# Attention on query blocks of 64 by key blocks of 128, with fp16 transposes, 1 KB loads and attention steps spread between MLP units

## The chip, the cores and the metric

The kernel runs on one core of one Trainium2 chip. The metric is the device time of one execution in microseconds (us). Each quoted time is the median of several executions, with their range. The span of a run, from its first to its last instruction, is 1.6 to 1.9 us shorter than its time. The profiled execution of before is not among its timed runs: its span of 415.4 us points to a time of about 417 us (an estimate), 1% above the median, so a difference of spans against before is off by some 2 to 4 us from the difference of the medians. A single core has no second die to compare with, so a run is called slow when it lies over 1.5% above the fastest of the same kernel; all profiled runs here were fast (for before by that estimate).

The engines are PE (matrix multiplications and transposes), DVE (vector), ACT (activation, exponentials and casts), GpSimd (called POOL in the trace) and SP, which issues DMA transfers. PSUM is the memory into which these kernels let PE write its results, and from which DVE and ACT take them; the other tiles lie in SBUF. The granted clock is the share of PE's full clock that the profile reports as let through by the throttle.

## The reference

There are 8 batches, 8 heads, 576 tokens and 64 elements per head. Attention is causal with a window of 64 tokens. Its result goes through a normalisation and an MLP of 512 to 2,048 to 512, and the attention output is added again.

```
pos = arange(576); rel = pos[:, None] - pos[None, :]
mask = (rel >= 0) & (rel < 64)
attn = softmax(where(mask, q @ k.T / 8, -1e9));  x = attn @ v      # as [8, 576, 512]
xn   = (x - mean) / sqrt(var + 1e-6) * g_ln
out  = x + relu(xn @ w_ch1) @ w_ch2
```

The 4,608 tokens form 36 blocks of 128, and four blocks form an MLP group, so there are nine groups and eight batches of attention.

## The kernel before

All inputs are loaded as fp32. The q and k loads take 256-byte runs (one token of one head). PE transposes the fp32 data, and DVE casts while it takes the result out of PSUM:

```
def emit_tr_burst(b, c):                       # c: chunk of 128 tokens
    for hp in range(H // 2):                   # a pair of heads
        tp = p_ps_att.tile([128, 2, 128], FP32, tag="att", ...)      # pool of 6 PSUM buffers
        nc.tensor.transpose(out=tp[:, 0, :nr], in_=qn[:nr, 2*hp:2*hp+2, :], ...)
        nc.tensor.transpose(out=tp[:, 1, :nr], in_=kn[:nr, 2*hp:2*hp+2, :], ...)
        nc.vector.tensor_copy(out=qkT[(b, hp)][:, :, s0:s0+nr], in_=tp[:, :, :nr])
```

Scores take 128 keys by up to 192 queries. V is cast by DVE, w1 and w2 by ACT. The MLP of a group is queued as 16 first-layer units and four second-layer units, and the emission order puts one to three units after each attention step (`filler(n)`). The weights arrive in the order in which the MLP wants them, with attention for batches 0 and 1 between:

```
for c in range(NCH):
    emit_loads_qk(0, c)
wdma(0, 1, 2, 3)                # w1 pieces on SP
...                             # V of batch 0
for c in range(NCH):            # batch 0, with w1 loads and casts between its blocks
    ...
    emit_block_pv(kblk)
    if kblk == 0: wcast(0, 1)
    elif kblk == 1: wcast(2, 3); wdma(4, 5)
    ...
```

A scheduler in the compiler may reorder the instructions of an engine; what is called the compiled order below is the result.

The softmax here doesn't subtract the row's maximum and nothing guards it: scores larger than these inputs give would overflow.

## Time and profile before

| | before |
|---|---|
| time, median of 3 runs | 413.38 us (413.15 to 414.93) |
| span of the profiled run | 415.4 us |
| first MLP matmul | 49.7 us |
| last output addition of MLP groups 0 to 8 begins at | 105.6, 158.9, 200.9, 240.9, 281.5, 322.5, 356.2, 383.9, 411.6 us |

These lines of the page of before are the span, the busy time of each engine, the busy tenths in 40 slices of 10.4 us, and the shares of the chain of work that ended last (followed back from the last instruction, at each step to what released it).

```profile
span 415.4 us, 7242 instructions
PE 375.3 (90%) x2768; PEld 195.4 (47%) x2768; DVE 236.2 (57%) x820; ACT 161.1 (39%) x337; POOL 37.8 (9%) x50
PE   2576559769999999999999999999999999999996
PEclk9999979987969999999999999999999999999999
DMA  9999998991791951496139133920002001102002
PE 72%; DMA 10%; ACT 7%; SPq 6%; DVE 4%; issue 1%; ACTq 0%
```

The DMA row is at 9 in most of the first nine slices, while PE is at 2 to 9: the start waits for loads. From the tenth slice on, PE is at 9.

The next lines are busy time by stretch in before. The columns are the window, its length, and the busy time and instruction count of PE, PEld, DVE, ACT and POOL, then the granted PE clock, the DMA share and the bandwidth.

```profile
core 0: us, PE busy (x) PEld busy (x) DVE busy (x) ACT busy (x) POOL busy (x), PEclk, DMA share, GB/s
47.00:106.00 59.00, 48.29 (x306) 22.41 (x305) 25.21 (x88) 30.41 (x62) 4.22 (x5) 0.88 0.80 196
106.00:159.00 53.00, 52.31 (x409) 28.11 (x408) 38.11 (x140) 19.42 (x44) 4.22 (x5) 0.94 0.68 132
...
201.00:241.00 40.00, 39.72 (x332) 20.95 (x326) 28.49 (x94) 18.80 (x44) 2.47 (x3) 1.00 0.46 103
...
357.00:384.00 27.00, 27.00 (x127) 12.25 (x126) 2.14 (x4) 9.55 (x16) 0.00 (x0) 1.00 0.11 39
```

Group 0 falls into a stretch of 59 us, starved of weights and at a granted clock of 0.88. A middle group takes 40 us and PE is busy for 39.7 of them. A late group, with no attention left, takes 27.7 us by the table.

### The profile page before, as it was taken

What the parts mean: (1) busy time and instruction counts of PE and PEld (TensorE: products, weight loads), DVE (VectorE), ACT (ScalarE), POOL (GpSimd) and SP (SyncE); (2) the same over time, 40 slices, a digit from 0 to 9 for tenths busy, and PEclk for the clock granted to TensorE, in tenths of its full rate; (3) what the DMA queues carried; (4) which work ended last, traced back from release to release, by engine and by line L of the source; (5) the groups of instructions that cost most, each with busy time, mean ns of one, the idle gap of its engine ahead of it and who ended that gap; (6) DMA issues with size and microseconds to landing.
All of it is one profiled execution on the core that took longest, in us unless ns stands there. A gap on an engine that the chain in (4) does not pass through costs nothing.

```text
span 415.4 us, 7242 instructions
## 1 busy us (share of the span) xinstructions
PE 375.3 (90%) x2768; PEld 195.4 (47%) x2768; DVE 236.2 (57%) x820; ACT 161.1 (39%) x337; POOL 37.8 (9%) x50
## 2 busy tenths in 40 slices
PE   2576559769999999999999999999999999999996
PEld 1355324424545654564465456545644544444442
DVE  3387803564758856885697579748856717102001
ACT  1152248931066226423545333533380450440620
POOL 8232100210011001300010020000000000000000
PEclk9999979987969999999999999999999999999999
DMA  9999998991791951496139133920002001102002
GB/s 180 210 243 238 191 235 236 251 214 61 163 163 33 178 134 52 114 184 148 51 95 195 62 109 79 152 76 28 2 1 77 27 0 51 52 0 77 25 27 76
DMA packets 90227, 46.62 MB, mean 112 GB/s; under 512 B 79312, under 2 KB 79312, under 8 KB 90192
## 3 DMA queue, kind: packets, MB, share of 16 engines
q1 hardware_dynamic: 85328, 36.71, 39.8%
q0 software_dynamic: 2784, 8.92, 9.2%
q10 hardware_dynamic: 2080, 0.52, 0.7%
q8 instruction: 22, 0.36, 0.4%
q14 instruction: 13, 0.11, 0.1%
HBM read 36.70 MB, written 9.44 MB: 111 GB/s over the span
## 4 chain that ended last, share of the span: by engine, by line
PE 72%; DMA 10%; ACT 7%; SPq 6%; DVE 4%; issue 1%; ACTq 0%
SPq L89 3%; DMA w2st_945<-in_moe_w_ch_dram 2%; SPq L88 2%; DMA w1s_541<-in_moe_w_ch_dram 2%; DMA w1s_367<-in_moe_w_ch_dram 2%; DMA w1s_125<-in_moe_w_ch_dram 1%; ACT w2s L141 1%; DMA w1s_694<-in_moe_w_ch_dram 1%; PE ch_1_1160 L174 1%; DMA w1s_654<-in_moe_w_ch_dram 1%; PE ch_0_2539 L174 1%; PE ch_0_4513 L174 1%; PE ch_2_3334 L174 1%; PE ch_0_3240 L174 1%; PE ch_2_3982 L174 1%; PE ch_0_3888 L174 1%
## 5 line engine op out<-in xcount | busy, mean ns | idle before, releaser
L162 PEld LDWEIGHTS <-w1g 128*128 128x128 f16 x576 | 53.7, 100 | 62.5 <-issue 15.6
L174 PEld LDWEIGHTS <-hrT_630 128*128 128x128 f16 x64 | 6.8, 107 | 13.2 <-issue 7.6
L179 DVE TENSOR_TENSOR osb_5225<-ch_0_5208,xn_4120 128x512 f32<-128x512 f32 x1 | 0.7, 692 | 16.7 <-PE ch_0_5208 L174 16.7
L179 DVE TENSOR_TENSOR osb_5401<-ch_0_5384,xn_4743 128x512 f32<-128x512 f32 x1 | 0.7, 692 | 16.7 <-PE ch_0_5384 L174 16.7
L174 PEld LDWEIGHTS <-hrT_5013 128*128 128x128 f16 x64 | 6.3, 98 | 7.5
L174 PEld LDWEIGHTS <-hrT_4730 128*128 128x128 f16 x64 | 6.3, 98 | 7.6
L174 PEld LDWEIGHTS <-hrT_4422 128*128 128x128 f16 x64 | 6.2, 98 | 6.7 <-issue 0.2
L174 PEld LDWEIGHTS <-hrT_3834 128*128 128x128 f16 x64 | 5.9, 98 | 7.0 <-issue 0.5
L174 PEld LDWEIGHTS <-hrT_3186 128*128 128x128 f16 x64 | 5.9, 98 | 6.8 <-issue 0.5
L174 PEld LDWEIGHTS <-hrT_2608 128*128 128x128 f16 x64 | 5.9, 98 | 6.6 <-issue 0.5
L174 PEld LDWEIGHTS <-hrT_1416 128*128 128x128 f16 x64 | 6.0, 98 | 6.4 <-issue 0.5
L174 PEld LDWEIGHTS <-hrT_1980 128*128 128x128 f16 x64 | 5.9, 97 | 6.5 <-issue 0.7
L214 ACT ACTIVATE pt_0_1419<-sc_0_0_0_1420 128x384 f16<-128x384 f32 x1 | 0.5, 490 | 21.0 <-PE sc_0_0_1_1424 L207 21.0
L174 PE MATMUL ch_0_1104<-w2s,hrT_630 128*128 128x512 f16 x16 | 5.2, 439 | 3.4 <-ACT w2s L141 3.4
L166 ACT ACTIVATE hrT_4730<-hps_0_5112 128x512 f16<-128x512 f32 x1 | 0.6, 597 | 15.7 <-PE hps_0_5112 L162 15.7
L174 PE MATMUL ch_1_1160<-w2s,hrT_630 128*128 128x512 f16 x16 | 6.3, 522 | 0.0
L166 ACT ACTIVATE hrT_5013<-hps_0_5288 128x512 f16<-128x512 f32 x1 | 0.6, 597 | 14.1 <-PE hps_0_5288 L162 14.1
L179 DVE TENSOR_TENSOR osb_5049<-ch_0_5032,xn_3528 128x512 f32<-128x512 f32 x1 | 0.7, 690 | 9.4 <-PE ch_0_5032 L174 9.4
L195 DVE CAST qkT_2_547<-tp_2_2_682 128x256 f16<-128x256 f32 x1 | 0.4, 425 | 9.1 <-PE tp_2_2_682 L194 9.1
L214 ACT ACTIVATE pt_0_190<-sc_0_0_0_191 128x384 f16<-128x384 f32 x1 | 0.5, 490 | 12.5 <-PE sc_0_0_1_195 L207 12.5
L162 PE MATMUL hps_2_656<-zT_581,w1g 128*128 128x512 f16 x4 | 1.9, 622 | 3.8 <-ACT hrT_630 L166 3.8
L166 ACT ACTIVATE hrT_4422<-hps_0_4669 128x512 f16<-128x512 f32 x1 | 0.6, 597 | 11.8 <-PE hps_0_4669 L162 11.8
(2695 smaller groups left out, 1173.9 us busy)
## 6 DMA issues: line engine op xcount, KB each, us to landing
vnat_0_127<-in_v_dram ACTq DMA_DIRECT2D x1, 256.0 KB, 4.6
qnat_0_98<-in_q_dram SPq DMA_DIRECT2D x1, 256.0 KB, 4.0
knat_0_99<-in_k_dram SPq DMA_DIRECT2D x1, 256.0 KB, 5.7
vnat_1_129<-in_v_dram ACTq DMA_DIRECT2D x1, 256.0 KB, 6.5
vnat_2_140<-in_v_dram POOLq DMA_DIRECT2D x1, 256.0 KB, 7.4
qnat_1_102<-in_q_dram SPq DMA_DIRECT2D x1, 256.0 KB, 10.8
vnat_3_142<-in_v_dram POOLq DMA_DIRECT2D x1, 256.0 KB, 8.8
knat_1_103<-in_k_dram SPq DMA_DIRECT2D x1, 256.0 KB, 10.5
```

The costliest lines, as they stand in the source:

```text
L88: nc.sync.dma_start(out=qn[:nr], in_=q[b, :, s0:s0 + nr, :].rearrange("h s d -> s h d"))
L89: nc.sync.dma_start(out=kn[:nr], in_=k[b, :, s0:s0 + nr, :].rearrange("h s d -> s h d"))
L141: nc.scalar.activation(out=w2s[:, hc, :], in_=w_data.pop(p), func=AF.Copy, bias=0.0, scale=1.0)
L162: nc.tensor.matmul(out=hps, lhsT=w1g[:, kc, 128 * hc:128 * (hc + 1)], rhs=zt[:, kc, :], start=(kc == 0), stop=(kc == NKC - 1),)
L166: nc.scalar.activation(out=hrT[:, hc, :], in_=hps, func=AF.Relu, bias=0.0, scale=1.0)
L174: nc.tensor.matmul(out=ch, lhsT=hrT[:, hc, 128 * kb:128 * (kb + 1)], rhs=w2s[:, hc, :], start=(hc == 0), stop=(hc == NHC - 1),)
L179: nc.vector.tensor_tensor(out=o, in0=ch, in1=x_norm[kblk][:, :, :].rearrange("p h d -> p (h d)"), op=ALU.add,)
L195: nc.vector.tensor_copy(out=qkT[(b, hp)][:, :, s0:s0 + nr], in_=tp[:, :, :nr])
L214: nc.scalar.activation(out=ptc[:nk, s0:s0 + 2, :nq], in_=sc[:nk, :, :nq], func=AF.Exp, bias=0.0, scale=scale,)
```

## The change

The change is a rewrite of the attention part and of the emission order. Its intent is less attention work on PE, fewer and longer loads, fewer casts on ACT and DVE, and attention steps spread evenly between smaller MLP units. Its core, with cuts:

```diff
+# q, k: partition p holds the four tokens 4p..4p+3, so one run is 1 KB; GpSimd casts them to fp16
+nc.sync.dma_start(out=t[:, :].rearrange("p h j d -> p h (j d)"),
+    in_=src[b, hs, 0:512, :].rearrange("h (p j) d -> p h (j d)", j=4))
+# v and w2 are cast by the DMA itself
+nc.gpsimd.dma_start(out=vA[b][:nr, c, :, 0:D], in_=v[b, :, 128*c:128*c+nr, :].rearrange("h s d -> s h d"))
+# V shifted by 64 rows, so that 128 keys around a query block are one operand
+def make_vB(b):
+    nc.vector.tensor_copy(out=vB[b][64:128], in_=vA[b][0:64])
+    nc.vector.tensor_copy(out=vB[b][0:64, 1:5], in_=vA[b][64:128, 0:4])
-tp = p_ps_att.tile([128, 2, 128], FP32, tag="att")         # 6 buffers, shared
+tp = ps_t.tile([128, 2, 4, 128], FP16, tag="tp")           # 1 buffer for all transposes
+for i in range(2):
+    for j in range(4):
+        nc.tensor.transpose(out=tp[:, i, j, :], in_=src[:, i, j], identity=ident16)
+for i in range(2):      # undo the order of tokens: j is the fastest index of the destination
+    nc.vector.tensor_copy(out=dst[:, hp, 0:512].rearrange("c (p j) -> c j p", j=4), in_=tp[:, i])
 ...                    # scores: 64 queries by 128 keys; mask of 64 columns used for all
+for i in range(4): w2_load(i)
+load_v(1, range(5))                     # behind w2 on GpSimd's queue
+for st in att_steps(0, 0): st()         # the whole attention of batch 0, no MLP beside it
+for i in range(16): w1_cast(i)
+for g in range(NGRP):                   # 32 units of a group; steps of batch g+1 spread over 28
+    units = mlp_units(g); steps = att_steps(g + 1, g + 1); span = 28
+    ...
```

## The prediction

> **What bounds it now.** The core's summary says PE 90% busy. Read by stage (busy time per window, and order of time on PE):
>
> - 0 to about 105 us: loads. The slices show DMA at 90% or more until about 93 us at 180 to 250 GB/s; the chain of waits runs through the w1 and w2 loads. PE is half busy. MLP group 0 ends at 105.5 us.
> - 159 to 322 us (groups 2 to 5): PE, busy 98 to 100%. One group takes 40 to 41 us.
> - Last two groups, no attention left: 27.7 us each. So the MLP costs 27.7 us per group and attention adds 12 to 13 us of PE time.
>
> **What the change does to PE per group.** From the timeline of before, a batch costs: fp32 transposes of q and k (0.11 to 0.165 us each) 5 to 6 us, zT transposes 2.1 us, scores 2.1 us, PV 2.9 us (0.65 us a block). After: 40 fp16 transposes (estimate 0.06 to 0.1 us each, as their evacuation is now batched) 3 us, zT 1.3, scores 2.5 (72 matmuls of 64 columns in place of 40 of up to 192), PV 2.0 (always 16 matmuls a block). Estimate 9 to 10 us, plus 1 to 2 us of stalls, since PSUM has one buffer for transposes and one for PV. Period 38.5 us (36 to 41) in place of 40 to 41: small gain. DVE and ACT stay well below: I sum about 24 us of DVE work per group (1,024-element mask about 0.6 us, zT copies 1.1 us, q/k copies 0.6 us).
>
> **What it does to the start.** Fewer bytes are wanted early (batches 0 and 1 and the weights, 15.5 MB), in longer runs. But the compiled order holds a trap: DVE builds the shifted V of batch 1 before it evacuates the first transpose of batch 0, and waits for V of batch 1. That load stands on GpSimd's queue behind all of w2. So 6.6 MB of that queue must land while SP's queue (q, k, w1) competes. The Trainium skill, "DMA: Bandwidth & Descriptors", section "Issuing engines are not separate DMA queues", says that both run on the same 16 engines and interleave; the trace agrees: 200 to 240 GB/s together in the first 30 us. About 13 MB at 230 to 260 GB/s: DVE starts batch 0 near 50 us (42 to 60). Batch 0's attention is then unfilled, some 20 to 24 us of DVE chain, so MLP starts near 74 us (before: near 47 us). But from there w1, w2 and batch 1 are present, so no group starves: group 0 ends near 113 us and group 1 near 151 us (before: 105.5 and 159).
>
> **Sum.** 74 + 7 x 38.5 + 2 x 27.7 + 1 = 400 us, less 2 us as the timed run is shorter than the profiled span: 398 us. Range 380 to 418. Chances: faster 0.64, same 0.28, slower 0.08.
>
> **What would show it.** First DVE copy out of a transpose at 42 to 60 us, preceded by a wait for a V load; first MLP matmul at 62 to 85 us; distance between the ends of groups 2 to 6 at 36 to 41 us; last two groups again 27.7 us each; q/k transposes paced at 0.06 to 0.1 us; PE idle in group periods 1 to 3 us, released by DVE.
>
> **What would make it wrong.** Casting DMA slower (or faster) than plain loads, moving the start by 10 us or more; GpSimd's queue winning more than half of the bandwidth (start near 60 us, total near 385); GpSimd casts and DVE slowing each other; stalls at the single transpose buffer stretching the period beyond 41 us, which takes the gain away.

## More of the kernel before

The granted PE clock dips to 6 or 7 tenths in three single slices: the sixth, where PE is half busy, and the tenth and twelfth, where PE is at 9.

Group 1 takes 53 us although PE is busy for 52.3 of them: it holds the q and k transposes of two batches (80 of the 320; groups 2 to 5 hold one batch each, group 6 none) at a clock of 0.94.

In the trace in order of time, this is how DVE took q and k transposes out of PSUM in before. The columns are start, duration, engine, line, operation and shapes.

```profile
140.03 0.41 DVE L195 CAST qkT_1_1786<-tp_1_1_1819 128x256 f16<-128x256 f32 x1
140.36 0.41 DVE L195 CAST qkT_2_1787<-tp_2_1_1823 128x256 f16<-128x256 f32 x1
```

Each copy of 256 elements per partition follows the one before by 0.33 us, and DVE waits for nothing.

## The result and the profile after

| | before | after |
|---|---|---|
| time, median of 4 runs | 413.26 us (413.15 to 414.93) | 459.85 us (458.88 to 460.65) |
| span of the profiled run | 415.4 us | 458.2 us |
| first MLP matmul | 49.7 us | 93.0 us |
| end of group 0 | 105.6 us | 139.3 us |
| group 1 | 53.3 us | 42.9 us |
| groups 2 to 6, each on average | 39.5 us | 43.3 us |
| groups 1 to 6 together | 250.6 us | 259.4 us |
| groups 7 and 8, each on average | 27.7 us | 27.8 us |

The ratio is 1.111, with a 95% interval from 1.108 to 1.114: the change is 11% slower. A ratio is the mean time of one kernel's fast runs over that of the other's of the same rounds, so it is not quite the ratio of the quoted medians.

An end of a group is read from the trace as the start of its last output addition; the length of a group is the distance between two of these. For example, these are the ends of groups 1 and 6 on DVE, in order of time, in before:

```profile
158.92 0.69 DVE L179 TENSOR_TENSOR osb_2065<-ch_3_2048,xn_1124 128x512 f32<-128x512 f32 x1 [1.10 <-PE ch_3_2048 L174]
...
356.23 0.69 DVE L179 TENSOR_TENSOR osb_5109<-ch_3_5092,xn_4052 128x512 f32<-128x512 f32 x1 [1.91 <-PE ch_3_5092 L174]
```

And in after:

```profile
182.20 0.69 DVE L296 TENSOR_TENSOR osb_1558<-ch_3_1541,xn_908 128x512 f32<-128x512 f32 x1 [0.63 <-PE ch_3_1541 L290]
...
398.72 0.68 DVE L296 TENSOR_TENSOR osb_4204<-ch_3_4187,xn_3390 128x512 f32<-128x512 f32 x1
```

The loss of 42.8 us of span is then 33.7 us up to the end of group 0, 8.8 us in groups 1 to 6, and 0.3 us behind them. Group 1 alone is 10.4 us shorter and groups 2 to 6 together are 19.2 us longer, but these two can't be compared one by one: before does the q and k transposes of two batches in group 1 and of none in group 6, after those of one batch in each. Groups 1 to 6 together hold the q and k transposes and the scores of six batches in both (before also transposes the MLP input of one or two groups more in them). Their busy time (columns as above), in before and then in after:

```profile
105.64:356.23 250.59, 248.68 (x2025) 131.88 (x2025) 176.65 (x628) 98.77 (x216) 15.21 (x18) 0.99 0.41 90
139.32:398.72 259.40, 230.90 (x1973) 113.88 (x1972) 178.92 (x360) 85.27 (x156) 43.16 (x50) 0.99 0.33 66
```

PE is busy for 17.8 us less there and stands idle for 28.5 us in place of 1.9.

The page of after, the same lines:

```profile
span 458.2 us, 6775 instructions
PE 345.0 (75%) x2768; PEld 171.8 (37%) x2768; DVE 246.1 (54%) x488; ACT 136.2 (30%) x241; POOL 80.3 (18%) x100
PE   0000037278997899799969997998899799999996
DMA  8999966714018801930192192011001000101101
PE 51%; DVE 32%; DMA 11%; issue 3%; ACT 2%; POOL 1%; DVEq 0%; POOLq 0%
```

PE's busy time fell by 30 us and the program still became 43 us longer, because PE now stands idle: for the first five slices altogether, and in every group. DVE's share of the chain of waits rose from 4% to 32% while its busy share fell. That is the mark of an engine that others wait for although it is half empty.

Busy time by stretch in after (columns as before):

```profile
26.00:56.00 30.00, 1.04 (x8) 0.77 (x8) 1.73 (x3) 7.00 (x10) 7.08 (x9) 1.00 1.33 265
56.00:93.00 37.00, 16.07 (x186) 11.95 (x187) 25.49 (x50) 5.10 (x10) 10.96 (x13) 1.00 0.68 84
...
183.00:227.00 44.00, 38.92 (x340) 19.28 (x338) 31.21 (x61) 14.52 (x27) 8.89 (x11) 1.00 0.48 92
227.00:269.00 42.00, 37.20 (x320) 18.44 (x318) 27.94 (x56) 13.97 (x26) 11.74 (x14) 1.00 0.52 98
```

Three losses can be read here. From 26 to 56 us no engine does much, although DMA moves 265 GB/s. From 56 to 93 us batch 0's attention runs with PE under half busy. In the groups PE is idle for 4.8 to 5.1 us of 42 to 44.

The first loss, DVE in order of time. The bracket is the idle time before and what ended it:

```profile
52.94 0.70 DVE L118 COPY vB_658<-vA_179 64x2080 f16<-64x2080 f16 x1 [27.98 <-DMA vA_179<-in_v_dram]
54.95 0.83 DVE L117 COPY vB_658<-vA_179 64x2600 f16<-64x2600 f16 x1 [1.31 <-DMA vA_179<-in_v_dram]
55.80 2.42 DVE L157 COPY qT_186<-tp_0_0_192 128x512 f16<-128x512 f16 x2
59.41 2.43 DVE L157 COPY kT_187<-tp_1_0_207 128x512 f16<-128x512 f16 x2 [1.20 <-PE tp_1_0_207 L154]
```

The compiled order put the shifted V of batch 1 ahead of the first copy of batch 0. DVE waits 28 us for it, and the transposes, scores and exponentials of batch 0 wait behind DVE. Batch 0's own shifted V stands before the copy as well and had already held DVE until 23.2 us. The longest waits of after say the same from the other side (engine and what waited, for whom, total, times, longest):

```profile
ACT pt_0_260 L187 <- PE sc_0_1_259 L180: 31.3, 1, 31.3
PE tp_1_0_207 L154 <- DVE qT_186 L157: 30.9, 1, 30.9
...
DVE vB_658 L118 <- DMA vA_179<-in_v_dram: 28.0, 1, 28.0
```

GpSimd has a second trap of the same kind. It issues the V loads of batch 1 before it casts q of batch 0, and some of these issues wait until a V load of batch 0 has landed:

```profile
23.32 1.92 POOL L110 DMA_DIRECT2D vA_179<-in_v_dram  x2 [2.68 <-DMA vA_115<-in_v_dram]
25.29 1.04 POOL L94 CAST c_0_0_0_188<-q_0_0_107 128x1024 f16<-128x1024 f32 x1
```

In after, this one was hidden behind the first.

The second and third losses start from the copies. A pair of copies takes 2.43 us, for 1,024 elements per partition. Before's copies took 0.33 us for 256 elements, so four of them would take 1.3 us. The transposes share one PSUM buffer, so PE cannot begin the next eight until the pair is done. PE in a group, in order of time:

```profile
96.31 0.63 PE L154 MATMUL tp_0_0_535<-ident_97,c_0_1_0_525 128*128 128x128 f16 x8
...
97.64 1.03 PE L277 MATMUL hps_3_556<-zT_479,w1g 128*128 128x512 f16 x4
99.57 0.61 PE L154 MATMUL tp_1_0_562<-ident_97,c_1_1_0_527 128*128 128x128 f16 x8 [0.91 <-DVE qT_523 L157]
...
102.80 0.61 PE L154 MATMUL tp_0_1_579<-ident_97,c_0_1_1_552 128*128 128x128 f16 x8 [1.11 <-DVE kT_524 L157]
```

The eight transposes themselves take 0.6 us. PE then does one or two MLP units and stands for about 1.1 us at the next transpose, four times a group (the fourth before the 64-token remainder).

### The profile page after: what moved, and what is told of

It reads as the page before. It is cut to its first block, busy times and chain, and to the rows that moved or that the text cites. A ratio compares the mean times of both kernels' runs of the same rounds, so it can differ in the third digit from the quotient of the medians.

```text
span 458.2 us, 6775 instructions
## 1 busy us (share of the span) xinstructions
PE 345.0 (75%) x2768; PEld 171.8 (37%) x2768; DVE 246.1 (54%) x488; ACT 136.2 (30%) x241; POOL 80.3 (18%) x100
## 3 DMA queue, kind: packets, MB, share of 16 engines
q0 software_dynamic: 39616, 6.82, 18.9%
## 4 chain that ended last, share of the span: by engine, by line
PE 51%; DVE 32%; DMA 11%; issue 3%; ACT 2%; POOL 1%; DVEq 0%; POOLq 0%
DMA vA_179<-in_v_dram 7%; DMA vA_115<-in_v_dram 4%; PE ch_0_1297 L290 1%; DVE qT_523 L157 1%; DVE kT_1569 L157 1%; DVE qT_2612 L157 1%; DVE kT_3147 L157 1%; DVE qT_1568 L157 1%; DVE qT_3146 L157 1%; DVE qT_2102 L157 1%; DVE kT_2613 L157 1%; DVE kT_524 L157 1%; DVE kT_2103 L157 1%; DVE kT_1059 L157 1%; DVE qT_1058 L157 1%
## 5 line engine op out<-in xcount | busy, mean ns | idle before, releaser
L277 PEld LDWEIGHTS <-w1g 128*128 128x128 f16 x576 | 53.3, 98 | 57.9 <-issue 2.6
L154 PE MATMUL tp_1_0_207<-ident_97,c_1_0_0_190 128*128 128x128 f16 x8 | 1.0, 305 | 30.9 <-DVE qT_186 L157 30.9
L154 PE MATMUL tp_0_0_192<-ident_97,c_0_0_0_188 128*128 128x128 f16 x8 | 1.0, 311 | 26.4 <-POOL c_0_0_0_188 L94 26.4
L118 DVE COPY vB_658<-vA_179 64x2080 f16<-64x2080 f16 x1 | 0.7, 697 | 28.0 <-DMA vA_179<-in_v_dram 28.0
L154 PEld LDWEIGHTS <-c_1_0_0_190 128*128 128x128 f16 x8 | 0.8, 136 | 31.2 <-issue 31.2
L118 DVE COPY vB_255<-vA_115 64x2080 f16<-64x2080 f16 x1 | 0.7, 697 | 21.6 <-DMA vA_115<-in_v_dram 21.6
L154 PEld LDWEIGHTS <-c_0_0_0_188 128*128 128x128 f16 x8 | 0.8, 142 | 26.4 <-POOL c_0_0_0_188 L94 26.4
L110 POOL DMA_DIRECT2D vA_1712<-in_v_dram x5 | 4.3, 861 | 29.9 <-PE tp_0_0_1070 L154 29.9
L110 POOL DMA_DIRECT2D vA_2756<-in_v_dram x5 | 4.2, 856 | 29.8 <-PE tp_0_0_2114 L154 29.8
L110 POOL DMA_DIRECT2D vA_2252<-in_v_dram x5 | 4.2, 866 | 28.2 <-PE ch_3_1541 L290 28.2
L290 PEld LDWEIGHTS <-hrT_4207 128*128 128x128 f16 x64 | 6.3, 98 | 7.5
L290 PEld LDWEIGHTS <-hrT_4384 128*128 128x128 f16 x64 | 6.3, 98 | 7.6
L110 POOL DMA_DIRECT2D vA_3296<-in_v_dram x5 | 4.2, 866 | 24.9 <-issue 24.9
L290 PEld LDWEIGHTS <-hrT_1051 128*128 128x128 f16 x64 | 6.0, 103 | 6.7 <-issue 1.6
L290 PEld LDWEIGHTS <-hrT_3139 128*128 128x128 f16 x64 | 5.8, 98 | 6.0
L290 PEld LDWEIGHTS <-hrT_3649 128*128 128x128 f16 x64 | 5.7, 98 | 6.1
L290 PEld LDWEIGHTS <-hrT_2095 128*128 128x128 f16 x64 | 5.8, 98 | 5.9
L290 PEld LDWEIGHTS <-hrT_2605 128*128 128x128 f16 x64 | 5.7, 98 | 6.0
L290 PEld LDWEIGHTS <-hrT_1561 128*128 128x128 f16 x64 | 5.7, 98 | 5.9
```

Of the source, the lines that this page charges most:

```text
L110: nc.gpsimd.dma_start(out=vA[b][:nr, c, :, 0:D], in_=v[b, :, 128 * c:128 * c + nr, :].rearrange("h s d -> s h d"),)
L118: nc.vector.tensor_copy(out=vB[b][0:64, 1:5], in_=vA[b][64:128, 0:4])
L154: nc.tensor.transpose(out=tp[:, i, j, :], in_=src[:, i, j], identity=ident16)
L277: nc.tensor.matmul(out=hps, lhsT=w1g[:, kc, 128 * hc:128 * (hc + 1)], rhs=zT[g][:, kc, :], start=(kc == 0), stop=(kc == NKC - 1),)
L290: nc.tensor.matmul(out=ch[kb], lhsT=hrT[:, hc, 128 * kb:128 * (kb + 1)], rhs=w2s[:, hc, :], start=(hc == 0), stop=(hc == NHC - 1),)
```

## The experiments

The theory after the result had two independent parts. One is the order at the start: V of batch 1 in the way of batch 0. The other is the copies that write with a step of 8 bytes (`"c (p j) -> c j p"`, four fp16 elements), together with the single PSUM buffer. The rivals were that the casting DMA, the 1 KB layout as such, or the spreading of steps is at fault.

Each experiment's ratio is to runs of before on the same chip, whose medians were 413.8 to 414.9 us.

### Copies that read with a stride and write contiguously

```diff
-out=dst[:, hp, 0:512].rearrange("c (p j) -> c j p", j=4), in_=tp[:, i],
+out=dst[:, hp, 0:512].rearrange("c (p j) -> c p j", j=4), in_=tp[:, i].rearrange("c j p -> c p j"),
```

> Only the eight copies a batch out of the q/k transposes change: the same permutation, but PSUM is read with the stride and SBUF is written contiguously. Theory A (the 8-byte step of the 2-byte WRITES makes these copies slow): a copy falls from 1.22 us to about 0.6 us, the cycle of one transpose step in a group from 3.23 to about 2.4 us, the group period from 43.4 to 38.5-40 us, and the start by about 5 us: total 420-432 us. Rival B (the 512-element fp16 copy out of PSUM costs this whatever the access, or the stride costs as much on the read side): a copy stays at 1.1 us or more and the total within 5 us of 460.

Measured: 425.96 us (424.25 to 428.0), ratio to before 1.030 (1.024 to 1.035). This one line is worth 34 us. The copies by form (busy time and mean ns of one, then the idle time before them):

```profile
L157 DVE COPY qT<-tp 128x512 f16<-128x512 f16 x32 | 20.6, 686 | 17.3 <-PE tp L154 17.3
```

A copy went from 1,320 to 686 ns and a pair from 2.43 to 1.29 us. The first copy still began at 56.7 us, so the start trap was untouched, and the groups went from 43.2 us to 38.5 us (ends of groups 0 and 6 at 132.1 and 363.1 us, divided by six). PE was idle only 0.5 to 0.8 us in windows of one group. The cost lies in the strided write: the same elements, moved with the stride on the PSUM side, take half the time.

### Loads in 256-byte runs again, copies contiguous on both sides

```diff
-nc.sync.dma_start(out=..., in_=src[b, hs, 0:512, :].rearrange("h (p j) d -> p h (j d)", j=4))     # cut
+for j in range(4):
+    nc.sync.dma_start(out=t[:, :, j, :], in_=src[b, hs, 128*j:128*j+128, :].rearrange("h p d -> p h d"))
-out=dst[:, hp, 0:512].rearrange("c (p j) -> c j p", j=4)
+out=dst[:, hp, 0:512].rearrange("c (j p) -> c j p", p=128)
```

> Undoes the 1 KB-run loads alone: q and k come in 256-byte runs, so rows are in order and the copies are contiguous on both sides. Theory A: a copy takes about 0.35-0.45 us, the group period is 38-39.5 us, the start is shorter by 6-7 us but for slower loads; total 415-428 us. Rival (the long runs are worth more than the copies cost): loads slow down and the total stays above 445 us.

Measured: 416.36 us (414.0 to 416.73), ratio 1.005 (1.000 to 1.010).

```profile
L158 DVE COPY kT<-tp 128x512 f16<-128x512 f16 x32 | 12.1, 420 | 19.7 <-PE tp L155 19.7
```

A copy took 420 ns and a pair 0.76 us. In the groups PE was idle 0.6 to 0.8 us, much as with strided reads. The rest of its gain came from elsewhere. DMA moved only 144 and 177 GB/s in the first two slices, against 211 and 241 in after, and V of batch 1 landed earlier, so that the first copy began at 40.2 instead of 55.8 us; that V came earlier because the q and k loads competed less with it is an inference. The Trainium skill, "DMA: Bandwidth & Descriptors", section "Specifications", gives 512 bytes as the least transfer for full rate; these rates agree in direction, but before moved 180 and 210 GB/s in its first two slices with 256-byte runs, so the length of the runs alone does not set the rate. With a trap at the start, slower q and k loads were a gain. With the trap gone they are a loss, as a later experiment shows.

### The order at the start, pinned

```diff
-nc.vector.tensor_copy(out=vB[b][64:128], in_=vA[b][0:64])
+tc.keep_in_program_order(nc.vector.tensor_copy(out=vB[b][64:128], in_=vA[b][0:64]))   # both copies
-load_v(1, range(5))            # before batch 0's attention steps
+load_v(1, range(5))            # after them, kept in program order on GpSimd
```

> Same instructions, two orders pinned: DVE builds the shifted V of batch 1 where the program has it, after batch 0, and GpSimd issues the load of V of batch 1 after its casts for batch 0. Theory C (order trap): the first DVE copy out of a transpose moves from 55.8 us to 14-20 us; ACT's w1 casts (until 38 us) then hold the first exp, so MLP starts at 58-66 us in place of 93 us; period unchanged at 43.4 us; total 425-435 us. Rival D (the start is bound by DMA bytes whatever the order): MLP starts no earlier than 83 us, total above 450 us.

Measured: 429.61 us (429.55 to 429.81), ratio 1.038 (1.034 to 1.042), so 30 us better than after. The first copy on DVE:

```profile
14.22 2.43 DVE L159 COPY qT<-tp 128x512 f16<-128x512 f16 x2 [12.70 <-PE tp L156]
```

It moved from 55.8 to 14.2 us, and the MLP from 93.0 to 62.1 us. The copies stayed at 1,318 ns, and the groups (ends of groups 0 and 6 at 106.9 and 368.7 us) stayed at 43.6 us. A new wait took 12.9 us of the win: the scores waited for the exponentials, and the first of these began at 39.7 us, because ACT first cast 16 pieces of w1, until 39.6 us. The pin also moved batch 0's own shifted V behind the copies, so the win is for both.

### Two PSUM buffers for the transposes

```diff
-ps_t  = ctx.enter_context(tc.tile_pool(name="pst",  bufs=1, space=PSUM))
-ps_mm = ctx.enter_context(tc.tile_pool(name="psmm", bufs=3, space=PSUM))
+ps_t  = ctx.enter_context(tc.tile_pool(name="pst",  bufs=2, space=PSUM))
+ps_mm = ctx.enter_context(tc.tile_pool(name="psmm", bufs=2, space=PSUM))
```

> A second PSUM buffer for transposes, taken from the MLP's three. Theory E (PE stalls in the groups because one transpose buffer is drained for 2.43 us before the next burst): the four or five stalls of 0.9-1.1 us a group mostly vanish, period 39.5-41 us, start 2-4 us shorter, total 435-445 us. Rival (DVE's order and its 2.43 us per pair set the pace, or two MLP buffers cost as much as they give): total within 8 us of 460, or slower.

Measured: 423.22 us (422.45 to 423.44), ratio 1.022 (1.017 to 1.027), which is better than expected.

```profile
L157 DVE COPY kT<-tp 128x512 f16<-128x512 f16 x32 | 39.7, 1338 | 2.8 <-PE tp L154 2.8
```

The copies are as slow as in after, and yet PE's waits for them are nearly gone: PE is idle 0.6 to 0.9 us in windows of 39 us. So slow copies alone do not cost time in the groups. Slow copies out of a single buffer do. Either half undone removes nearly the whole loss there (groups 1 to 6 take 39.2 us each here and 38.5 us with strided reads, against 43.2), so the two gains must not be added.

### Only the DVE half of the order

This is after with the two shifted-V copies kept in order, and V of batch 1 left where it was on GpSimd.

> The changed kernel with DVE's order alone pinned (GpSimd's order as it was, strided writes as they were). Tells which of the two pins of the third experiment did it. Theory: DVE's wait was the blocking one; GpSimd's casts still start at 25 us, so the first copy comes at 27 us, the last at 42 us, MLP starts at 62-67 us: total within 5 us of the third experiment (430). Rival (GpSimd's order was what held the start): total above 445 us.

Measured: 433.01 us (431.57 to 433.86), ratio 1.045 (1.041 to 1.049). It is 3.4 us slower than with both pins. The first copy began at 28.2 us, behind the GpSimd casts, but the exponentials began at 42.5 us, only 2.8 us later than with both pins. DVE's order was the blocking one; GpSimd's was nearly hidden by the w1 casts on ACT.

### Both corrections

This is the pinned order together with the strided reads.

> The first and the third experiment together (strided reads instead of strided writes; the two orders pinned). If the two causes are separate terms they add: first copy at 14 us, MLP still starts at 60-63 us because ACT's w1 casts hold the first exp until 39 us, period 38.6 us; total 394-402 us, faster than before (413). If they overlap (rival: one bottleneck seen twice), the total stays at 410 us or more.

Measured: 398.18 us (397.04 to 400.13), ratio 0.961 (0.957 to 0.966). From after this is 61.7 us; the two alone gave 33.9 and 30.2 us. They nearly add (64.1 us), so they are separate causes. The largest wait of PE was then 17.0 us for the exponentials, which stood behind the w1 casts: first exponential at 38.8 us.

### And the w1 casts moved

Only six w1 casts stand before batch 0's exponentials. The other ten follow one by one between its later steps. The w1 staging pool grew from six to seven buffers.

```diff
-for st in att_steps(0, 0): st()
-for i in range(16): w1_cast(i)
+for i, st in enumerate(att_steps(0, 0)):
+    if i == 8:
+        for w in range(6): w1_cast(w)          # all casts kept in program order
+    st()
+    if 8 <= i < 18: w1_cast(i - 2)
```

> The fifth, with ACT's order mended as well: only the first six w1 casts stand before batch 0's exps, the other ten between them (one more w1 staging buffer). Theory: the start was three in-order queues blocked by work for later; MLP starts at 46-54 us in place of 62, period 38.6 us; total 381-392 us. Rival: w1 and w2 loads now bind (15 MB at 230-260 GB/s are there only at 58-65 us), so that what the start wins is lost again as PE waits for casts in group 0, and the total is within 5 us of the fifth's.

Measured: 384.43 us (382.67 to 385.95), ratio 0.928 (0.923 to 0.932). This beats both kernels: 7% faster than before and 16% faster than after. The first exponential began at 24.3 us and the MLP at 49.4 us:

```profile
24.25 0.65 ACT L189 ACTIVATE pt<-sc 64x256 f16<-64x256 f32 x2 [0.93 <-PE sc L182]
```

Where this version wins against before can be read from the group ends:

| | before | this version |
|---|---|---|
| end of group 0 | 105.6 us | 90.2 us |
| group 1 | 53.3 us | 38.0 us |
| groups 2 to 6 together | 197.3 us | 195.6 us |
| groups 1 to 6 together | 250.6 us | 233.6 us |
| groups 7 and 8 together | 55.4 us | 55.6 us |

The busy time of groups 1 to 6 in this version:

```profile
90.19:323.76 233.57, 230.31 (x1978) 115.03 (x1977) 156.96 (x362) 85.50 (x156) 46.08 (x50) 0.99 0.37 73
```

Of the 32 us of span, 15.4 us are won up to the end of group 0, where before waited for weights (PE idle for 10.3 of its 56.0 us from the first MLP matmul on, at a clock of 0.88), and 17.0 us in groups 1 to 6, where neither version waits for weights. There PE's busy time falls from 248.7 to 230.3 us. An estimate puts 3 us of this down to the clock of 0.94 in before's group 1 (0.06 of the 52.6 us that PE was busy there). The cleanest pair is groups 2 to 5, which hold the q and k transposes of four batches in both: 163.5 us before and 155.6 us here, 2.0 us a batch. (This is an estimate too: before's four groups also hold half a batch of scores more.) From the last groups of 27.7 us one can work out what the attention of a batch adds there: before (163.5 - 4 x 27.7) / 4 = 13.2 us, here 11.2 us.

### Two PSUM buffers on top

This is the version at 384 us with two transpose buffers.

> The sixth with a second PSUM transpose buffer from the MLP's three. With copies of 0.6 us the stall before a burst is already nearly gone, so the theory says: within 4 us of the sixth, either way. Rival (the single buffer still costs): 6 us or more faster.

Measured: 383.71 us (380.66 to 385.52), ratio 0.925 (0.920 to 0.931): the same within the spread. Once the copy is short, the second buffer buys nothing, as the experiment on the buffers alone implied.

### 256-byte runs in the corrected order

This has the order and the w1 casts of the version at 384 us, with the loads and copies of the experiment on 256-byte runs.

> The orders pinned as in the sixth, but 256-byte runs and contiguous copies in place of 1 KB runs and strided reads. Contiguous copies (0.36 us) save DVE time that is not on PE's path in the groups, so the period is 38.6-38.9 us as in the sixth; the start has slower q/k loads (about 170 GB/s in place of 250 at first): MLP starts 3-10 us later than in the sixth, total 3-10 us slower than it.

Measured: 395.82 us (393.86 to 397.52), ratio 0.954 (0.948 to 0.959). The groups pace much as in the version at 384 us (groups 1 to 6 take 38.5 us each, against 38.9), and the loss of 11.4 us, slightly more than expected, is all in the start (group 0 ends 15.3 us later): the transposes wait for the casts, whose q and k loads land late (29.1 us in five waits, against 13.5 us in one), the first exponential begins at 38.1 us and the MLP at 60.9 us. So the 1 KB runs are a real gain, as long as the scatter that they bring is put on the side where it is cheap.

### Steps in a burst

The attention steps of a batch are finished within the first 8 units of a group, and no longer spread over 28 (`span = 8`).

> The sixth experiment with the attention steps of a group handed out among its first 8 MLP units in place of the first 28. Tells what the spreading is worth. If spreading hides the waits of a step for DVE and ACT behind MLP matmuls, the burst brings PE stalls of 2-5 us a group: total 396-420 us. Rival (the scheduler moves the steps back between units by itself, or the waits are short): total within 5 us of the sixth (384).

Measured: 400.54 us (396.35 to 403.52), ratio of fast runs 0.960 (0.954 to 0.966). Two of its four runs count as slow, with granted clocks of 0.966 and 0.956; the two fast runs are 396.35 and 398.71 us, about 13 us above the mean of the spread version. The total lies where it was expected, but not for the reason given: there is no new long wait of PE, and in groups 1 to 6 it was idle for 3.6 us in all, against 3.3 us in the spread version. Groups 1 to 6 took 41.0 us each, against 38.9. Three of them contain a stretch of lowered clock and averaged 42.4 us; the other three averaged 39.6 us. One such stretch of this run, by windows of 3 us:

```profile
108.00:111.00 3.00, 3.00 (x40) 1.31 (x38) 2.72 (x6) 2.22 (x4) 0.00 (x0) 0.53 0.00 0
111.00:114.00 3.00, 3.00 (x28) 1.39 (x22) 2.19 (x4) 1.19 (x2) 0.00 (x0) 0.50 0.02 5
```

The column after the five engines is the granted clock. All four runs of this kernel had mean clocks from 0.956 to 0.978, all four of the spread one from 0.991 to 1.000, so the lower clock goes with the burst. The two were run on different chips, but the version with V loaded plainly (next), which is spread and ran on the chip of the burst, had clocks from 0.985 to 0.999. Why bursts of small matmuls should bring it about is not shown. In sum, spreading is worth about 13 us, by this estimate two thirds of it through the clock (three times 2.8 us).

### V loaded plainly and cast by DVE

V comes as fp32 through the same queue into staging tiles, and five DVE copies cast it. Room for the staging was taken from other pools (one V buffer, one normalised block and one w1 piece fewer).

> The sixth experiment with the cast of V taken out of the DMA: plain fp32 loads on the same queue into staging tiles, five DVE copies a batch (0.4 us each), 4 staging kilobytes traded against one V buffer and one xn buffer. The DMA time of the software queue falls from 24.4% of the span (93 us of 16 engines) to 50-60 us, as V's packets are whole 256-byte or longer ones and no longer 128 bytes. In the groups DMA does not bind, and DVE has 2 us more to do out of 38: total within 8 us of the sixth (384), more likely slower. Rival (casting DMA held the kernel back): 8 us or more faster.

Measured: 401.5 us (397.28 to 402.55), ratio 0.968 (0.960 to 0.975). The expectation missed: it is 17 us slower, where at most 8 us had been expected. The queue lines say what the transfers with the cast in DMA cost. Columns are packets, megabytes and share of 16 engines' span; first the version at 384 us:

```profile
q0 software_dynamic: 39616, 6.82, 24.4%
```

And with V loaded plainly:

```profile
q0 software_dynamic: 5056, 11.54, 12.9%
```

That is 93.5 against 51.4 us of DMA time, so the casting transfers, which also come in smaller packets, are dearer. But DMA does not bind in the groups, and in the start other waits grew: the MLP began at 56.8 us, since the remainder transposes waited 5.7 us for GpSimd casts and the exponentials began at 32.5 us. Because the edit also shifted the compiled order and took buffers away, this run does not price the cast by itself. That the cast in DMA is not needed to explain after's loss is shown by the version at 384 us, which keeps it and is faster than before; how much it lengthened the wait for V in after's start was not tested.

## Why the prediction was wrong

What was right:

- What bounded before, and the late groups: predicted 27.7 us each, measured 27.8.
- The trap at the start: DVE waits for V of batch 1, first copy predicted at 42 to 60 us, measured at 55.8. The two queues moved 211 to 279 GB/s together in the first five slices, near the 230 to 260 of the estimate. That they share the same engines and interleave is what the cited section of the skill states; the sum agrees with it but does not test it. Taking the trap away gave 30 us, near what the prediction charged for it (74 less 47 us), but by luck in part: the first copy came 41.6 us earlier, and the w1 casts on ACT decided how much of this got through.
- That no group would wait for weights: in after's group 0 PE waits for copies. Group 1 was predicted at 38 us and measured at 42.9; its 53.3 us before were no starvation, as PE was busy for 52.6 of them.
- PE idle in groups released by DVE, and transposes at less than 0.1 us each (eight in 0.61 us).

What failed, as steps of the sum (the predicted span is 400 us, the measured 458.2 us, 58 us apart; the 2 us that the prediction took off for the timed run go the other way in after, whose timed run is 1.7 us longer than its span):

1. "q/k copies 0.6 us". A copy took 1.32 us alone and 1.2 us in a pair. The estimate took the number of elements and ignored the 8-byte step of the write. Strided reads measured 0.69 us and contiguous copies 0.42 us. DVE's work per group, summed to 24 us in the prediction, was 28 to 33 us.
2. "plus 1 to 2 us of stalls". PE was idle about 4.8 us a group. The prediction's list of dangers did name the single transpose buffer, but costed it with the short copy. Slow copies and one buffer together make the loss; undoing either one removes nearly all of it.
3. "PE ... 9 to 10 us" for the attention of a batch. With the stalls gone it measured 11.2 us, about 0.5 us of it idle, against 13.2 us before. So the size was off by 1 to 2 us, while a saving on PE, as forecast, is there: about 2 us a batch where some 3 had been expected. The groups of that version take 38.9 us each. Steps 2 and 3 together made groups 1 to 6 43.2 us each where 38.5 were predicted: 28 us.
4. "some 20 to 24 us of DVE chain". From the first copy to the first MLP matmul it took 37.1 us: 14.1 us for four transpose steps of 3.6 us and the remainder, and 23.1 us for everything behind them. The chain was counted as DVE work, but it is a ping-pong of PE, DVE and ACT in which each waits for the others. Strided reads shortened it to 32.6 us, so the copies are only a third of this miss; the rest was not taken apart further. With the first copy at 55.8 us this put the first MLP matmul at 93.0 instead of 74 us, and group 0, slower than the estimate by 7 us as well, ended at 139.3 instead of 113 us: 26 us.

The remaining 3 us are at the end. The range was too narrow because steps 1 and 2 were treated as small and independent, while both hang on one line of code.

## What to carry to other kernels

When a layout trick makes loads longer, look where its scatter ends up, and cost that instruction by its access pattern and not by its elements: here one line, with the stride on the write or on the read, was worth 34 us. Read the compiled order of each engine for instructions of the next batch that stand before the first ones of this batch, and pin them; a half-empty engine with a growing share of the chain of waits is the sign. And before comparing two schedules stretch by stretch, count which work falls into each: before's group 1 looked starved at 53 us and was a busy group with two batches of transposes. With that counted, the attention rewrite saved about 2 us a batch once its stalls were gone, and having the weights in time about 15 us, all up to the end of group 0.

## What the Trainium skill lacked or had wrong

- "SBUF — State Buffer", section "Door 1: The DMA port swizzle", says in its note on cachelines that one can stride for free up to 8 bf16 elements (16 bytes), needing two hits per line. A DVE copy of 512 fp16 elements that writes with a step of 4 elements has two hits per line, and took 1.32 us, against 0.69 us with the stride moved to the PSUM read and 0.42 us contiguous on both sides. For these DVE writes this was not free.
- "VectorE: DVE Perf Modes", section "What auto-detection actually checks", asks for 16-bit tensors with a step of 1 or -1 throughout for the doubled rate with one port. The strided read (0.69 us) against the contiguous copy (0.42 us) agrees. The page has nothing on a strided write being slower still than a strided read (1.32 against 0.69 us for the same elements).
- "TensorE: Matmul & The Clock Gate", Part 1, has the clock halve after about 3.4 us of idle PE. Before shows a stretch that fits: PE busy 0.9 of 4 us from 54 to 58 us, then a granted clock of 0.50 from 58 to 62 us. Two other stretches the page's idle rule does not explain: the burst kernel shows half clock from 108 to 114 us after 9 us in which the trace has PE busy without a gap, and before a clock of 0.54 from 117 to 122 us after 11.4 us in which PE was busy for 10.8. (The ends of matmuls are modelled in these traces, so gaps too short to show can't be excluded.)
- "DMA: Bandwidth & Descriptors", section "SWDGE vs HWDGE vs iDMA", says which engine can issue casting transfers but not what they cost: with V cast in flight the software queue took 93.5 us of DMA time for 39,616 packets, with V plain 51.4 us for 5,056; the share of the cast and that of the smaller packets were not taken apart.
